# Hash bits by way of DRAM in ScalarE's queue, weight exponents in halves, and two pairs of heads in another order

## The chip, the cores and the metric

One core of a Trainium2 chip runs the kernel in one launch. The metric is the device time of one execution in microseconds (us). The engines are TensorE (PE in the profile), VectorE (DVE), ScalarE (ACT), GpSimd (POOL) and SyncE (SP); each works through its own instructions in the order in which the program gives them, and engines wait for each other by semaphores. DMAs are issued here from SP, ScalarE and GpSimd.

## The reference

```python
def _attn_ref(q, k, v, proj):                 # q, k, v: (4, 8, 768, 64); proj: (64, 6)
    q_bits = (np.einsum('bhsd,dk->bhsk', q, proj) > 0).astype(np.int64)
    k_bits = (np.einsum('bhsd,dk->bhsk', k, proj) > 0).astype(np.int64)
    powers = 2 ** np.arange(n_bits)
    mask = np.sum(q_bits * powers, -1)[:, :, :, None] == np.sum(k_bits * powers, -1)[:, :, None, :]
    scores = np.where(mask, scale * np.matmul(q, k.transpose(0, 1, 3, 2)), -1000000000.0)
    attn = np.exp(scores - np.max(scores, axis=-1, keepdims=True))
    attn = attn / (np.sum(attn, axis=-1, keepdims=True) + 1e-09)
    return np.matmul(attn, v).astype(np.float32)

def _moe_ref(x, w_in, w_out):                 # x: (3072, 512); w_in: (512, 2048); w_out: (2048, 512)
    r = np.maximum(x @ w_in, 0.0)
    return ((r * r) @ w_out).astype(np.float32)
```

A query attends only to the keys with the same six sign bits. The attention's output, heads side by side, is the input `x` of a layer with a squared ReLU. The two weight matrices arrive as 64-bit floating-point numbers.

## The kernel before

The kernel has two halves. The first computes the attention of the 32 heads, two heads (a pair `pr`, 0 to 15) at a time, and writes `x` to DRAM. The second is the layer with the squared ReLU, by products of blocks that save multiplications; the change does not touch it.

**One pair.** Scores are computed with keys on the partitions. A half-score `score(pr, kt, i)` (L442) is for key block `kt` (0 to 5, 128 keys) and half `i` of the queries (384): TensorE multiplies first the hash bits of keys and queries (`marks`, bf16) and then the features (`own`, fp32) into one PSUM tile `st` for both heads (`products`, L426). The bits are scaled so that a pair of query and key with different bits gets a score so negative that its exponential is 0. ScalarE then takes the exponential into the tile `e` (`weight`, L437). `st` comes from `turn` (L105), a ring of two PSUM buffers, which the projections of the hash (`hash_bits`, L358) use too. So a half-score can start only when the exponential of the half-score two turns back is done. `attend(pr, kt, s)` (L494) multiplies `e` by the values into `xo`; `attend_whole` (L510) does both of its halves at once. VectorE adds the `e` tiles into `total` (`add_up`, L465); `sum_up`, `invert`, `spread` and `normalize` (L525 to L591) turn that into the divisor and apply it to `x_raw`, ScalarE's copy of `xo` (`keep_x`, L516). `sum_up` and `spread` use `spare`, one more PSUM buffer.

**The hash bits of the next pair.** While a pair is scored, `hash_bits(pr + 1)` projects the next pair's features, `signs` (L383) turns that into scaled signs by two operations of ScalarE into the tile `signed`, whose rows are ordered by queries or keys, half and bit. `place_bits` (L391) copies them to the rows of the tiles `bits` where `products` reads them, by eight DMAs in SP's queue, seven partitions each. SP's queue also carries the loads of queries and keys (`qk_nat`, L307, eight per pair), of values (`v_nat`, L316) and of weights (`raw`, L141), the writes of `x_t` (L591) and of the block sums of the weights (`w_in<-s_in`, L219), and from pair 13 on the blocks `w_unit` (L656). GpSimd loads `x` (L640) from pair 12 on.

**The weights.** Beside the attention the 64-bit weights are rounded to 32 bits, one piece per pair. VectorE cuts out the exponent (`part_power`, L146), ScalarE shifts it to its place by two operations over 2 x 512 elements per partition (`place_power`, L157), VectorE takes the rest (`part_top`, L167) and puts both together (`round_weight`, L183).

**The order** is written out by hand in the loop over the pairs (L687 to L773): half-scores and attends alternate, and the other steps stand between them. For pair 0 the hash of pair 1 stands behind its first four half-scores, and VectorE makes pair 1's features (`features(1)`, L351) just before. After the last pair come its last two `attend_whole`, the divisor and the last sums of `x` (L774 to L788).

Of the kernel before, what the change touches and what calls it, by code (L numbers as in the profile page):

```python
# [9 lines left out]
BF16 = mybir.dt.bfloat16  # L10
# [24 lines left out]
def kernel(  # L35
# [120 lines left out]

    def place_power(i):  # L157


        if i not in parts:  # L160
            return
        power = parts[i]
        small = p_w.tile([P, 2, PIECE], U8, name="small", bufs=1)
        nc.scalar.activation(out=small, in_=power, func=ACTF.Relu, bias=excess)  # L164
        nc.scalar.activation(out=power, in_=small, func=ACTF.Copy, scale=2.0**23)  # L165
# [49 lines left out]
    def put_factor(n, c, t):  # L215
# [27 lines left out]
    signed = const.tile([P, 2, HS], BF16, name="signed")  # L243
    all_bits = [
        [const.tile([P, S], BF16, name=f"bits{w}_{i}") for w in range(2)] for i in range(2)
    ]

    def constants():
# [10 lines left out]
        for r in range(0, P, NR_B):  # L259
            nc.vector.memset(lifts[r:r + N + 1], 1.0)  # L260
            nc.vector.memset(lifts[r:r + N], -SMALL)
            if r >= 2 * NR_B:
                nc.vector.memset(gains[r:r + N + 1], -FAR / 2 * N)
                nc.vector.memset(gains[r:r + N], FAR / 2)
        for pair in all_bits:
            for t in pair:
                nc.gpsimd.memset(t, 0.0)
        nc.vector.memset(ones, 1.0)
# [103 lines left out]
    def first_signs(w):  # L372

        bits[0, w] = t = all_bits[0][w]
        for c in range(2):
# [7 lines left out]
    def signs(pr):  # L383


        nc.scalar.activation(
            out=signed, in_=hashed[pr, 0][:, :, 0:HS], func=ACTF.Sign, scale=HUGE, bias=lifts
        )
        nc.scalar.activation(out=signed, in_=signed, func=ACTF.Copy, scale=gains)

    def place_bits(pr):  # L391

        for w in (1, 0):
            bits[pr, w] = t = all_bits[pr % 2][w]
            for c in range(2):
                at = (2 * w + c) * NR_B
                for h in range(2):
                    nc.sync.dma_start(  # L398
                        out=t[h * D:h * D + NBITS + 1, c * HS:(c + 1) * HS],
                        in_=signed[at:at + NBITS + 1, h],  # L400
                    )

    def first_keys(c, banks):

        if c == 0:
            bits[0, 1] = all_bits[0][1]
        t = bits[0, 1]
# [257 lines left out]
    with tc.manual_schedule():  # L665
# [21 lines left out]
        for pr in range(NP):  # L687
# [72 lines left out]

            score(pr, 4, 0)
            attend(pr, 2, 1)
            score(pr, 4, 1)
# [19 lines left out]
        for n in (2, 3):  # L783
            sum_x(0, n)
        spread(pr)
        normalize(pr)
# [797 lines left out]
```

## Time and profile before

| | us |
|---|---|
| median of 3 runs | 888.74 |
| lowest and highest run | 888.21, 891.19 |
| the profiled execution | 888.8 |
| its span, from the first instruction to the last | 886.9 |

The profile is of one execution. A row of the timeline gives the start (us from the span's start), the duration, engine, line, operation, tiles, shape and count, and in brackets the idle time of the engine before it and what ended it. A row of a wait gives the engine, line and tile that waited, what for, and the total, the number of times and the longest in us. A row of a group gives busy time and mean duration (ns) of one, then the idle time ahead of it. A row of one line's instructions gives minimum, median and maximum in ns. A row of the DMA chain gives the start, the time from the issue to the use, and the tiles. A row of a stretch gives its bounds and length, the busy time of PE, PEld (TensorE's loading of weights), DVE, ACT and POOL, then the granted share of TensorE's clock, the DMA engines' busy share and GB/s.

### The profile page before, as it was taken

How to read it: one execution, taken by the hardware profiler on the slowest of the kernel's cores; microseconds unless marked ns; L12 is line 12 of the kernel's file. 1: busy time of each engine (PE TensorE's matmuls, PEld its weight loads, DVE VectorE, ACT ScalarE, POOL GpSimd, SP SyncE). 2: the span in 40 equal slices, each digit the busy share in tenths (PEclk: the TensorE clock that was granted, in tenths of full speed). 3: DMA queues.
4: the chain of work that ended last, by engine and by line, in shares of the span. 5: the costliest groups of instructions: out<-in, count | busy, mean ns of one | idle time of the engine just before them, and what ended most of it. 6: DMA issues, size and time to landing. Idle time of an engine off the chain costs nothing.

```text
span 886.9 us, 16832 instructions
## 1 busy us (share of the span) xinstructions
PE 861.4 (97%) x6612; PEld 539.3 (61%) x6612; DVE 751.6 (85%) x1021; ACT 347.2 (39%) x552; POOL 123.6 (14%) x232
## 2 busy tenths in 40 slices
PE   7999999999989999999999999999999999999996
PEld 3555555555545554444588875556888755568885
DVE  4899999998978988888779978888889788888875
ACT  5777767776756662222211113332111133321110
POOL 1000000000000000554213121111100211110002
PEclk9999999999999999999999999999999999999998
DMA  9667897988887732999788874446756745454565
GB/s 206 120 123 155 205 178 161 191 202 184 187 213 166 261 100 92 332 291 292 253 325 268 240 181 145 165 130 226 277 161 174 184 141 168 130 166 145 165 170 106
DMA packets 224422, 168.03 MB, mean 189 GB/s; under 512 B 164904, under 2 KB 182640, under 8 KB 224336
## 3 DMA queue, kind: packets, MB, share of 16 engines
q1 hardware_dynamic: 189424, 87.84, 41.2%
q0 software_dynamic: 12528, 41.30, 14.9%
q10 hardware_dynamic: 22384, 37.76, 13.9%
q8 instruction: 53, 0.87, 0.4%
q14 instruction: 33, 0.27, 0.1%
HBM read 124.52 MB, written 41.68 MB: 187 GB/s over the span
## 4 chain that ended last, share of the span: by engine, by line
PE 84%; DMA 5%; ACT 5%; DVE 2%; SPq 2%; issue 1%; ACTq 0%; DVEq 0%
PE acc L812 39%; PE acc L1031 15%; PE st L432 12%; PE xo L488 8%; PE acc L984 5%; ACT e L438 2%; DMA raw<-in_moe_w_out_dram 2%; DMA bits<-signed 2%; ACT power L165 1%; PE tot L537 1%; ACT small L164 1%; SPq L307 1%; PE hash L367 1%; SPq L398 1%; DMA v_nat<-in_v_dram 1%; DVE total L475 1%
## 5 line engine op out<-in xcount | busy, mean ns | idle before, releaser
L438 ACT ACTIVATE e<-st 128x768 f32<-128x768 f32 x192 | 153.6, 809 | 94.7 <-PE st L432 83.7
L432 PE MATMUL st<-feat 64*64 64x384 f32 x1536 | 163.0, 485 | 1.0 <-DVE feat L336 1.0
L488 PE MATMUL xo<-e,v_nat 64*64 64x385 f32 (+1 forms) x1520 | 163.3, 487 | 0.5 <-DMA v_nat<-in_v_dram 0.5
L812 PE MATMUL acc<-b,leaf 128*128 128x256 f32 x600 | 133.0, 379 | 0.0
L812 PEld LDWEIGHTS acc<-b,leaf 128*128 128x128 f32 x600 | 113.9, 190 | 16.0 <-issue 0.6
L475 DVE TENSOR_TENSOR total<-total,e 128x1536 f32<-128x1536 f32 x64 | 111.6, 1743 | 5.1 <-ACT e L438 5.1
L488 PEld LDWEIGHTS xo<-e,v_nat 64*64 64x64 f32 (+1 forms) x1520 | 63.8, 133 | 56.0 <-issue 43.9
L1031 PE MATMUL acc<-t_x,w_unit 128*128 128x512 f32 x192 | 90.2, 592 | 0.0
L432 PE MATMUL st<-bits,bits 64*64 64x384 bf16 x768 | 70.7, 328 | 9.3 <-DMA bits<-signed 6.3
L432 PEld LDWEIGHTS st<-feat 64*64 64x64 f32 x1536 | 61.7, 133 | 29.7 <-issue 25.1
L812 PE MATMUL acc<-t,leaf 128*128 128x256 f32 x336 | 76.3, 380 | 0.0
L812 PEld LDWEIGHTS acc<-t,leaf 128*128 128x128 f32 x336 | 63.6, 190 | 9.3 <-DVE t L602 0.5
L896 DVE SCALAR_TENSOR_TENSOR b<-h 128x512 f32<-128x512 f32 x96 | 65.7, 691 | 3.0
L432 PEld LDWEIGHTS <-bits 64*64 64x64 bf16 x768 | 29.5, 107 | 52.7 <-issue 46.5
L1031 PE MATMUL acc<-x,w_unit 128*128 128x512 f32 x128 | 60.1, 592 | 0.0
L483 POOL MEMSET token<- 1x1 f32 x62 | 16.6, 269 | 309.1 <-PE xo L488 258.6
L812 PE MATMUL acc<-x,w_unit 128*128 128x512 f32 x128 | 56.5, 593 | 0.0
L1031 PEld LDWEIGHTS acc<-t_x,w_unit 128*128 128x128 f32 x192 | 36.5, 190 | 28.9 <-issue 26.8
L812 PE MATMUL acc<-b_t,leaf 128*128 128x256 f32 x240 | 53.8, 379 | 0.0
L812 PEld LDWEIGHTS acc<-b_t,leaf 128*128 128x128 f32 x240 | 45.5, 190 | 6.2
L819 ACT COPY two<-acc 128x256 f32<-128x256 f32 (+1 forms) x29 | 12.5, 432 | 87.9 <-PE acc L812 75.4
L819 ACT COPY one<-acc 128x256 f32<-128x256 f32 (+1 forms) x29 | 12.5, 432 | 82.2 <-PE acc L812 53.5
(159 smaller groups left out, 1181.6 us busy)
## 6 DMA issues: line engine op xcount, KB each, us to landing
leaf<-w_out ACTq DMA_DIRECT2D x142, 256.0 KB
w_unit<-w_in SPq DMA_DIRECT2D x16, 640.0 KB
raw<-in_moe_w_in_dram SPq DMA_DIRECT2D x8, 1024.0 KB
raw<-in_moe_w_out_dram SPq DMA_DIRECT2D x8, 1024.0 KB
w_unit<-w_in SPq DMA_DIRECT2D x8, 896.0 KB
w_out<-sums POOLq DMA_DIRECT2D x16, 448.0 KB, 6.9
sum<-w_in SPq DMA_DIRECT2D x16, 448.0 KB
v_nat<-in_v_dram SPq DMA_DIRECT2D x16, 384.0 KB
```

Source lines behind the costliest of these rows:

```text
L164: nc.scalar.activation(out=small, in_=power, func=ACTF.Relu, bias=excess)
L165: nc.scalar.activation(out=power, in_=small, func=ACTF.Copy, scale=2.0**23)
L432: nc.tensor.matmul(out=st[k * HK:(k + 1) * HK, h, 0:HS], lhsT=src[1][rows, key], rhs=src[0][rows, cut], start=first, stop=not first, skip_ ...
L438: nc.scalar.activation(out=key_of(pr, kt)[:, :, i, 0:HS], in_=st[:, :, 0:HS], func=ACTF.Exp, scale=scale)
L475: nc.vector.tensor_tensor(out=totals[pr], in0=totals[pr], in1=e, op=ALU.add)
L483: step = nc.gpsimd.memset(token, 0.0)
L488: return nc.tensor.matmul(out=outs[pr][h * D:(h + 1) * D, c, 0:HS + 1], lhsT=nat[pr, "v_nat"][rows, h, kt * D:(kt + 1) * D], rhs=key_of(pr ...
L812: nc.tensor.matmul(out=acc[to], lhsT=a(i), rhs=b(i), start=first and i == 0, stop=last and i == n - 1, skip_group_check=True,)
L819: nc.scalar.copy(out=t, in_=acc[of])
L896: nc.vector.scalar_tensor_tensor(out=out, in0=h, scalar=0.0, in1=h, op0=ALU.max, op1=ALU.mult)
L984: nc.tensor.matmul(out=out, lhsT=w[:, a], rhs=b, start=start, stop=stop, skip_group_check=True)
L1031: nc.tensor.matmul(out=acc[to], lhsT=w[:, PLACE[a], f], rhs=bt[b](f), start=first and f == 0, stop=last and f == NFT // 2 - 1, skip_group_ ...
```

## The change

1. `signed` is written to a new DRAM tile `bits_d` by one DMA in ScalarE's queue, right behind the two operations of `signs`. `place_bits` reads it back with two DMAs in ScalarE's queue, one per head, each of seven partitions and four pieces (queries and keys, two halves). They stand behind `score(pr, 4, 0)` and no longer right behind `signs`. The tiles of bits are merged, one for queries and keys together, in place of two.
2. `place_power` works on one half of the piece (512 elements) per call. From pair 1 on the first half stands behind `attend(pr, 1, 0)` and the second where the whole stood; in pair 0 both halves stand where the whole stood.
3. In pair 0, `attend(0, 0, 0)`, `score(0, 2, 0)`, `attend(0, 1, 0)` and `score(0, 2, 1)` move ahead of the hash of pair 1.
4. In the last pair, `score(15, 5, 1)` takes the spare PSUM buffer, `attend(15, 2, 0)` moves behind `add_up(15, 4)`, and the last `attend_whole` and `keep_x` move behind the sums of the divisor and `invert`.

```diff
-    def place_power(i):
+    def place_power(i, g):
         if i not in parts:
             return
-        power = parts[i]
-        small = p_w.tile([P, 2, PIECE], U8, name="small", bufs=1)
+        power = parts[i][:, g]
+        small = p_w.tile([P, PIECE], U8, name="small", bufs=1)
         nc.scalar.activation(out=small, in_=power, func=ACTF.Relu, bias=excess)
         nc.scalar.activation(out=power, in_=small, func=ACTF.Copy, scale=2.0**23)
...
-    all_bits = [
-        [const.tile([P, S], BF16, name=f"bits{w}_{i}") for w in range(2)] for i in range(2)
-    ]
+    all_bits = [const.tile([P, 2, S], BF16, name=f"bits{i}") for i in range(2)]
+    bits_d = p_d.tile([P, 2, HS], BF16, name="bits_d")
...
-        for pair in all_bits:
-            for t in pair:
-                nc.gpsimd.memset(t, 0.0)
+        for t in all_bits:
+            nc.gpsimd.memset(t, 0.0)
...
         nc.scalar.activation(out=signed, in_=signed, func=ACTF.Copy, scale=gains)
+        nc.scalar.dma_start(out=bits_d, in_=signed)
...
     def place_bits(pr):
-        for w in (1, 0):
-            bits[pr, w] = t = all_bits[pr % 2][w]
-            for c in range(2):
-                at = (2 * w + c) * NR_B
-                for h in range(2):
-                    nc.sync.dma_start(
-                        out=t[h * D:h * D + NBITS + 1, c * HS:(c + 1) * HS],
-                        in_=signed[at:at + NBITS + 1, h],
-                    )
+        t = all_bits[pr % 2]
+        src = bits_d.rearrange("(g r) h c -> h r g c", r=NR_B)
+        for h in range(2):
+            nc.scalar.dma_start(
+                out=t[h * D:h * D + NBITS + 1].rearrange("r w (c n) -> r (w c) n", c=2),
+                in_=src[h, 0:NBITS + 1],
+            )
+        for w in range(2):
+            bits[pr, w] = t[:, w]
...
-    def score(pr, kt, i):
+    def score(pr, kt, i, st=None):
...
-        st = turn("st")
+        st = st or turn("st")
...
             else:
                 keep_x(old)
                 sum_up(old, 0)
-            if more:
-                hash_bits(pr + 1, turn("hash"))
-                signs(pr + 1)
-                place_bits(pr + 1)
-            if pr > 0:
-                if not more:
+                if more:
+                    hash_bits(pr + 1, turn("hash"))
+                    signs(pr + 1)
+                else:
                     score(pr, 2, 0)
                 sum_up(old, 1)
                 invert(old)
...
             part_power(pr)
+            if pr == 0:
+                attend(pr, 0, 0)
             if more:
                 score(pr, 2, 0)
-            attend(pr, 0, 0)
+            if pr > 0:
+                attend(pr, 0, 0)
+            else:
+                attend(pr, 1, 0)
             score(pr, 2, 1)
-            attend(pr, 1, 0)
+            if pr > 0:
+                attend(pr, 1, 0)
+                place_power(pr, 0)
+            else:
+                hash_bits(1, turn("hash"))
+                signs(1)
             score(pr, 3, 0)
...
                 normalize(old)
-                place_power(pr)
+                place_power(pr, 1)
             add_up(pr, 3)
...
             score(pr, 4, 0)
+            if more:
+                place_bits(pr + 1)
             attend(pr, 2, 1)
             score(pr, 4, 1)
             attend(pr, 3, 1)
...
             score(pr, 5, 0)
-            attend(pr, 2, 0)
-            score(pr, 5, 1)
+            if more:
+                attend(pr, 2, 0)
+            score(pr, 5, 1, spare("st") if not more else None)
             attend(pr, 3, 0)
             if pr == 0:
-                place_power(0)
+                for g in range(2):
+                    place_power(0, g)
             add_up(pr, 4)
         pr = NP - 1
-        for kt in (SB - 2, SB - 1):
-            attend_whole(pr, kt)
-        keep_x(pr)
+        attend(pr, 2, 0)
+        attend_whole(pr, SB - 2)
         sum_x(0, 1)
         add_up(pr, SB - 1)
...
         invert(pr)
         for n in (2, 3):
             sum_x(0, n)
+        attend_whole(pr, SB - 1)
+        keep_x(pr)
         spread(pr)
         normalize(pr)
```

More of the change, by code (lines that the diff above doesn't have):

```diff
@@ L372, in first_signs @@
     def first_signs(w):
-        bits[0, w] = t = all_bits[0][w]
+        bits[0, w] = t = all_bits[0][:, w]
         for c in range(2):
@@ L389, in signs @@
         nc.scalar.activation(out=signed, in_=signed, func=ACTF.Copy, scale=gains)
+        nc.scalar.dma_start(out=bits_d, in_=signed)
     def place_bits(pr):
-        for w in (1, 0):
-            bits[pr, w] = t = all_bits[pr % 2][w]
-            for c in range(2):
-                at = (2 * w + c) * NR_B
-                for h in range(2):
-                    nc.sync.dma_start(
-                        out=t[h * D:h * D + NBITS + 1, c * HS:(c + 1) * HS],
-                        in_=signed[at:at + NBITS + 1, h],
-                    )
+        t = all_bits[pr % 2]
[7 more added lines that the diff above has]
+            bits[pr, w] = t[:, w]
     def first_keys(c, banks):
         if c == 0:
-            bits[0, 1] = all_bits[0][1]
+            bits[0, 1] = all_bits[0][:, 1]
         t = bits[0, 1]
```

## The prediction

> **What bounds the kernel now.** I read the page's totals first, then what TensorE waited for, then one pair of heads in the timeline, then the DMA issues.
>
> ```profile
> span 886.9 us, 16832 instructions
> PE 861.4 (97%) x6612; PEld 539.3 (61%) x6612; DVE 751.6 (85%) x1021; ACT 347.2 (39%) x552; POOL 123.6 (14%) x232
> ...
> PE st L432 <- DMA bits<-signed: 6.3, 8, 2.6
> PE st L432 <- ACT e L438: 3.1, 15, 0.3
> PE hash L367 <- DVE feat L351: 1.7, 1, 1.7
> ...
> PE xo L488 <- DMA v_nat<-in_v_dram: 0.5, 1, 0.5
> ```
>
> TensorE is busy in 97% of the span, so an edit pays only where TensorE waits, and the change touches only the attention half (up to 341 us). The list of its waits names four there: hash bits that land late, exponentials that come late, the hash of pair 1, and one load of values. Ends of matmuls are modelled, so I price the waits by spacings. The Sign operation (L386) comes once per pair, so its starts are a clock; of pairs 2, 9, 10, 11, 12 and 13:
>
> ```profile
> 57.10 0.90 ACT L386 ACTIVATE signed<-hash,lifts 128x768 bf16<-128x768 f32 x1 [0.33 <-PE hash L367]
> ...
> 194.96 0.90 ACT L386 ACTIVATE signed<-hash,lifts 128x768 bf16<-128x768 f32 x1 [0.33 <-DMA qk_nat<-in_q_dram]
> 215.91 0.90 ACT L386 ACTIVATE signed<-hash,lifts 128x768 bf16<-128x768 f32 x1 [0.34 <-PE hash L367]
> 236.20 0.90 ACT L386 ACTIVATE signed<-hash,lifts 128x768 bf16<-128x768 f32 x1 [0.34 <-PE hash L367]
> 261.03 0.90 ACT L386 ACTIVATE signed<-hash,lifts 128x768 bf16<-128x768 f32 x1 [0.34 <-PE hash L367]
> 282.99 0.90 ACT L386 ACTIVATE signed<-hash,lifts 128x768 bf16<-128x768 f32 x1 [0.34 <-PE hash L367]
> ```
>
> From pair 2 to 9 a pair takes (194.96 - 57.10)/7 = 19.69 us. The next four take 20.95, 20.29, 24.83 and 21.96, which is 1.26 + 0.60 + 5.14 + 2.27 = 9.3 us too much. These are the late bits, with what follows: after the longest wait the clock was granted at half for a while.
>
> ```profile
> 254.00:256.00 2.00, 2.00 (x18) 1.46 (x14) 1.80 (x3) 0.81 (x1) 0.00 (x0) 0.50 1.05 376
> ```
>
> (The 0.50 is the clock.) Now one steady pair, number 4, on ScalarE and TensorE:
>
> ```profile
> 97.39 0.94 ACT L389 ACTIVATE signed<-signed,gains 128x768 bf16<-128x768 bf16 x1
> 99.53 0.33 PE L432 MATMUL st<-bits,bits 64*64 64x384 bf16 x4
> 99.75 0.70 DVE L151 TENSOR_SCALAR power<-raw 128x1024 uint32<-128x1024 uint32 x1
> ...
> 102.69 0.34 PE L432 MATMUL st<-bits,bits 64*64 64x384 bf16 x4
> 103.00 1.14 ACT L164 ACTIVATE small<-power,excess 128x1024 uint8<-128x1024 uint32 x1
> 104.14 0.34 PE L432 MATMUL st<-bits,bits 64*64 64x384 bf16 x4
> 104.17 1.06 ACT L165 ACTIVATE power<-small 128x1024 uint32<-128x1024 uint8 x1
> 105.14 1.50 ACT L438 ACTIVATE e<-st 128x768 f32<-128x768 f32 x2
> 105.98 0.36 PE L432 MATMUL st<-bits,bits 64*64 64x384 bf16 x4 [0.20 <-ACT e L438]
> 107.43 0.36 PE L432 MATMUL st<-bits,bits 64*64 64x384 bf16 x4
> 108.50 0.81 ACT L438 ACTIVATE e<-st 128x768 f32<-128x768 f32 x1 [0.64 <-PE st L432]
> 108.89 0.36 PE L432 MATMUL st<-bits,bits 64*64 64x384 bf16 x4
> ```
>
> Half-scores start every 1.45 us (102.69 to 104.14; 107.43 to 108.89), but 104.14 to 105.98 is 1.84: **0.38 us lost**. The cause: two `turn` buffers, so score(5,0) at 105.98 needs the exponential of (4,0), and ScalarE ran both operations of `place_power` ahead of it. An exponential can start 1.07 us after its half-score starts (107.43 to 108.50) and takes 0.81, or 0.75 back to back; its buffer is wanted again 2.9 us after that start. So ScalarE may be about 1.0 us late before TensorE stops; `place_power` makes it about 1.4 late.
>
> **The change, part by part.**
>
> *1. Four smaller operations (L163 to L165).* Each half has 512 elements. The same engine's copies give the slope:
>
> ```profile
> L1039 ACT COPY two<-acc 128x512 f32<-128x512 f32 x16 | 9.4, 586 | 24.4 <-PE acc L1031 24.4
> L819 ACT COPY two<-acc 128x256 f32<-128x256 f32 x21 | 7.8, 373 | 65.1 <-PE acc L812 52.6 <-DMA leaf<-w_out 6.3 <-DVE h L599 3.1
> ```
>
> (586 - 373)/256 = 0.83 ns per element, so an operation of 1.06 us becomes 1.06 - 512 x 0.83 ns = 0.63, a half is 1.27 us, and ScalarE does 0.4 more per pair in all. The first half moves between the exponentials of (2,1) and (3,0); the second stays. In pairs 1 to 14 the 0.38 goes if nothing new comes: 14 x 0.38 = **5.3 us**. Pair 0 keeps its halves together at its end, and pair 15 is bound by VectorE (part 4).
>
> *2. Three DMA issues on ScalarE.* Eight issues leave SP; one write of `signed` to DRAM and two reads arrive in ScalarE's instruction stream.
>
> ```profile
> L398 SPq DMA_DIRECT2D bits<-signed x120: 688/689/1303, 23.6 to 311.1; - x120
> L1098 ACTq DMA_DIRECT2D leaf<-w_out x142: 326/327/702, 438.2 to 867.6; - x142
> ```
>
> The write has 128 rows like L1098, the reads have seven partitions like L398: 0.33 to 0.70 and 0.69 to 1.30 us each. I take 0.33 and 0.69, the medians, as the nearest rows. Walk through pair 4, its stall taken out: the write waits for `signed` (97.39 + 0.94 = 98.33), so exp(2,0) runs 98.7 to 99.5 and score(3,0) wants its buffer at 99.53: no wait, or 0.35 at 0.70. `part_power` ends at 99.75 + 0.70 = 100.45, then half a `place_power` to 101.7, exp(3,0) to 102.45 (wanted 102.69), exp(3,1) to 103.2, second half to 104.45, exp(4,0) to 105.2 (wanted 105.60). The reads wait for nothing fresh, so they can issue beside exp(4,0), 104.5 to 105.9; behind them queues exp(4,1), ending at 106.65, wanted at 107.05 by score(5,1). So at medians nothing stalls, with 0.1 to 0.4 us to spare. Between nothing and 0.35 at the write, and nothing and 0.8 at the reads, I take 0.15 us per pair: **-2.1 us** over 14 pairs, so 3.2 is left of part 1.
>
> The read also waits, on ScalarE, for the write to land; 98.7 to 104.5 is the cover.
>
> *3. The bits arrive by another queue.* Today they queue on SP behind weights and loads:
>
> ```profile
> 29.08 2.63 DMA bits<-signed
> ...
> 206.83 1.77 DMA bits<-signed
> ...
> 247.88 5.61 DMA bits<-signed
> ```
>
> From issue to use 1.77 us in a quiet stretch (0.69 of it issue), 2.63 beside loads, 5.61 beside a 2 MB load of `x`. Write: 5.8 us of cover, enough by all three. Reads: the second issues at about 105.2 and pair 5 wants it at 108.89 - 0.38 = 108.5, so 3.3 us: enough for the first two, not the third. What made bits late at pairs 9 to 13 was the issue: SP reached them late.
>
> ```profile
> 202.04 6.95 SPq L398 DMA_DIRECT2D bits<-signed  x8
> ...
> 268.32 7.73 SPq L398 DMA_DIRECT2D bits<-signed  x8
> ```
>
> The signs there ended at 196.8 and 262.9 (start + 0.90 + 0.94), so 5 us went by before SP reached the first issue and 7 to 8 in the eight issues, which ended at 209.0 and 276.0. ScalarE's reads issue 6.2 to 7.6 us after the signs (as in the walk through pair 4) and land by 205.5 and 271.6; the next pair wants them 12.0 us after its signs began (96.5 to 108.5 in pair 4), at 207.0 and 273.0. The longest wait stood beside POOL's load of `x`:
>
> ```profile
> 246.36 0.91 POOL L640 DMA_DIRECT2D x<-x_all  x1 [0.26 <-DMA raw<-in_moe_w_out_dram]
> ...
> 294.01 0.91 SPq L656 DMA_DIRECT2D w_unit<-w_in  x2
> ```
>
> The reads of that pair (238.0 + 6.2, to 245.6) issue before it. But what frees SP also moves the two `w_unit` loads from 294.0 to about 288, beside the reads of pair 13. Of 9.3 us I keep 1.5 for such collisions: **+7.8**, bounds 2 and 9.3. Every SP issue behind the eight (`x_all`, `v_nat`, eight `qk_nat`) also moves up by about 5 us (8 x 0.69), so the late `v_nat` of pair 14 (0.5) is early: **+0.6**.
>
> *4. First and last pair.* Pair 0 today waits 1.73 us for VectorE's `features(1)`; now two attends and two half-scores stand before the hash: +1.7, if `v_nat` has landed by about 15 us, 3.6 earlier than it is used now (the list has no wait for it there; bounds 0 and 1.7). But score(3,0) then follows score(2,1) by only the hash (0.64), with no attend between, and wants the buffer of exp(2,1), which ends 1.07 + 0.81 after score(2,1) starts: 1.88 - 1.45 = 0.4 lost, and about 0.2 behind the signs. Net **+1.1**. In the last pair VectorE is the chain:
>
> ```profile
> 323.70:338.90 15.20, 13.93 (x168) 6.98 (x164) 14.99 (x15) 8.66 (x11) 0.18 (x2) 1.00 0.13 45
> ...
> 338.92 0.86 PE L537 MATMUL tot<-total,ones 128*32 128x192 f32 x16 [1.02 <-DVE total L475]
> 340.95 0.50 PE L571 MATMUL tot<-both,picks 64*64 64x24 f32 x4 [1.18 <-DVE both L560]
> ```
>
> VectorE works 14.99 of 15.20 us up to the last `add_up`. Moving `attend_whole` (1.3 us) into the 1.18 wait fills a hole whose end VectorE sets: **+0.2**, bounds 0 and 1.0. The spare PSUM buffer and the merged memsets cost nothing: both are ready long before use.
>
> Sum: 5.3 - 2.1 + 7.8 + 0.6 + 1.1 + 0.2 = **12.9 us**. The profiled execution took 888.8 us (span 886.9 and 1.9 around it), as the median of 888.74. Forecast: 888.8 - 12.9 = 875.9, say **876 us**. VectorE does not bite before: in pair 4 it idles 1.24 of 19.70 us, and part 1 asks 0.23.
>
> **Rivals.**
>
> *A. ScalarE's issues take the place of the stall: slower.* Exp(4,1) may start by 106.3, so two reads from 104.5 on fit up to 0.9 us each. SP's issues of `qk_nat`, which move to the same moment, can be long, and if ScalarE's have to wait for them, the reads do:
>
> ```profile
> 499.28 18.28 SPq L1129 DMA_DIRECT2D out_dram<-h  x16
> ```
>
> Against: beside these 16 issues (1.14 us each) ScalarE's issues stayed within 0.70. For: 0.40 us of slack at 0.69, and L398's own 1.30. At 1.30 the reads end at 107.1 and exp(4,1) 0.8 too late; with the write at 0.70 a pair loses 1.0 us instead of 0.38: 14 x 0.6 = 9 more than now; if the reads also wait for exp(4,0) to end (0.75 more), 1.77: 14 x 1.4 = 19. With the other gains (9.7) that is 888 to 898, say 893. Slower from 1.1 us of stall per pair.
> By the Trainium skill's "Perfetto Trace Analysis", "DMA Instruction — HWDGE (DVE, Sync)", the descriptor generator is locked for exclusive use while one sequencer issues, which is this rival's mechanism. The row above speaks against a long lock.
>
> *B. The bits stay late.* The reads share DMA engines with what SP now sends earlier, at the same time. If the two long stalls (5.14 + 2.27, of which I had given up 1.5) stay, it is 888.8 - 12.9 + 5.9 = 882; if besides each pair waits 0.35 us, 887. For: 5.61 us beside one load. Against: today's stalled pairs begin with a late issue.
> The skill's "DMA: Bandwidth & Descriptors", "Issuing engines are not separate DMA queues", says that DMAs of all issuing engines interleave on the same engines and only issue time is saved; by it the 5.61 would remain and the time would be this rival's 882.
>
> **How the numbers follow.** Forecast 0.62 (870 to 881), B 0.20 (882 to 887), A 0.16 (888 to 898), better than 870 0.02. About 0.3% (2.7 us) is what a measurement of this kernel tells from no change: faster, below 886.1, holds the forecast and most of B, 0.79; within 0.07; slower 0.14, nearly all of A. The range from 870 to 889 leaves out the worse part of A and the 0.02.
>
> **What would show it.** Right: signs every 19.4 to 19.6 us from pair 2 to 14, no pair over 20.5; waits of TensorE for `bits` under 2 us; hash of pair 1 without a wait; `small` twice per pair at about 0.7 us. A: issues on ScalarE's queue over 0.9 us and "ACT e" the longest wait. B: "DMA bits" still there, with pairs 11 and 12 above 21 us. Wrong altogether: a period above 19.7 with neither wait, or a second half that takes longer than before from the last `spread` on.

## The result and the profile after

| us | before | after |
|---|---|---|
| median of 4 runs each, on one chip | 889.97 (888.21 to 894.74) | 881.6 (881.1 to 882.96) |
| the profiled execution's span | 886.9 | 879.7 |

The ratio is 0.99, with a 95% interval from 0.9858 to 0.9942: faster by 1%, 8.4 us in the medians and 7.2 in the profiled spans, where 12.9 had been forecast (876 us). The time lies in the forecast's range (870 to 889) and at the figure of rival B (882), but B's reason is only part of it.

The changed kernel's page begins with these totals:

```profile
span 879.7 us, 16684 instructions
...
PE 859.9 (98%) x6612; PEld 538.5 (61%) x6612; DVE 751.6 (85%) x1021; ACT 353.0 (40%) x584; POOL 123.8 (14%) x230
```

TensorE's waits in the changed kernel (total, times, longest, us):

```profile
PE st L431 <- ACT e L437: 3.9, 3, 2.5
PE st L431 <- DMA bits<-bits_d: 2.4, 5, 0.7
PE tot L536 <- DVE total L474: 1.9, 1, 1.9
```

The waits for the hash of pair 1 and for `v_nat` are gone. The wait for bits fell from 6.3 to 2.4, but the wait for exponentials, which had been fifteen short stops of at most 0.3 us, is now one of 2.5 and two short ones. ScalarE's timeline shows where. These are the Sign operations (now L384) in pairs 9 to 14, named by the pair that is being scored, with what follows the one in pair 12; the starts are again the clock of the pairs:

```profile
191.97 0.90 ACT L384 ACTIVATE signed<-hash,lifts 128x768 bf16<-128x768 f32 x1 [0.32 <-PE hash L365]
212.22 0.90 ACT L384 ACTIVATE signed<-hash,lifts 128x768 bf16<-128x768 f32 x1 [0.33 <-PE hash L365]
231.59 0.90 ACT L384 ACTIVATE signed<-hash,lifts 128x768 bf16<-128x768 f32 x1 [0.32 <-PE hash L365]
250.95 0.90 ACT L384 ACTIVATE signed<-hash,lifts 128x768 bf16<-128x768 f32 x1 [0.32 <-PE hash L365]
251.88 0.94 ACT L387 ACTIVATE signed<-signed,gains 128x768 bf16<-128x768 bf16 x1
255.33 0.35 ACTq L388 DMA_DIRECT2D bits_d<-signed  x1
255.79 1.51 ACT L437 ACTIVATE e<-st 128x768 f32<-128x768 f32 x2 [2.97 <-DMA qk_nat<-in_k_dram]
...
275.83 0.90 ACT L384 ACTIVATE signed<-hash,lifts 128x768 bf16<-128x768 f32 x1 [0.33 <-PE hash L365]
296.43 0.90 ACT L384 ACTIVATE signed<-hash,lifts 128x768 bf16<-128x768 f32 x1 [0.33 <-PE hash L365]
```

A pair now takes 19.36 us where nothing disturbs it (231.59 to 250.95), against 19.69 before. But pair 12 (250.95 to 275.83) takes 24.88, pair 13 takes 20.60, and pair 9 (191.97 to 212.22) 20.25. The long one has a visible cause. `signed` is done at 252.82, yet its write to DRAM, the next instruction of ScalarE, starts at 255.33, and the exponentials queued behind it have stood 2.97 us when they start. The row names a load of keys as what ended the idle time, and that load has nothing to do with `signed`.

The chain of waits of the changed kernel, in order of time, confirms it, and goes on to the reads of these bits:

```profile
243.91 3.98 SPq L305
...
247.93 2.90 SPq L305
...
250.88 4.39 DMA qk_nat<-in_k_dram
255.27 0.03 ACTq L388
...
255.33 0.35 ACTq L388
...
263.81 0.27 ACTq L395
...
264.12 4.41 DMA bits<-bits_d
```

Two issues of keys on SP took 3.98 and 2.90 us beside GpSimd's 2 MB load of `x`; the load of keys issued next, at 250.88, landed at 255.27, and ScalarE's write was let go in the same moment. The write then needed 8.2 us to land (263.55 by the trace's semaphore updates), so the first read went out at 263.81, 12.9 us after the Sign, where a quiet pair has it out at 7.5. The last read was used at 264.12 + 4.41 = 268.53, 17.58 us after the Sign; the next pair wants it 12.06 after (12.0 in the prediction's walk). These 5.52 us are the pair's whole loss, so it is still paid as late bits: TensorE's stop for the exponentials lies inside it. By the same reckoning, with the landings from the semaphore updates, late bits are 8.4 of the 8.8 us that all pairs lose. After TensorE's stop of 2.5 us its clock was granted at half (third column from the end), as in the stretch of the kernel before:

```profile
258.00:260.00 2.00, 2.00 (x20) 1.25 (x19) 1.99 (x2) 1.27 (x2) 0.00 (x0) 0.50 0.89 266
```

The built program's list of waits says why a write of bits should wait for a load of keys. It is no profile; the rows are ScalarE's write and reads of that pair, and SP's loads of queries and keys ahead of the write:

```
ScalarE  bits_d<-signed        waits DMAHW3, DMAHW5, DMAHW2, Activation
ScalarE  bits<-bits_d          waits DMAHW6, DMAHW2
ScalarE  bits<-bits_d          waits DMAHW0
SP       qk_nat<-in_q_dram x4  wait  DMAHW2 | DMAHW4 | DMAHW6 | DMAHW7
SP       qk_nat<-in_k_dram x4  wait  DMAHW0 | DMAHW1 | DMAHW2 | DMAHW3
```

SP's and ScalarE's DMAs share eight completion counters (semaphores that a landing counts up), handed out in turn in the program's order. Each DMA waits until the last user of its counter, about the eighth DMA before it, has landed. The write's own counter is DMAHW2, which the third load of keys has, exactly eight DMAs earlier; in the trace both count on the same semaphore. The second read of bits lists no wait but its counter's. The kernel before has the same rule, but its ScalarE issued no DMA between the first loads and the second half, so in the attention only SP ever stood in this line.

The span can be cut by starts that every trace has: the Sign in pair 1, the Sign in pair 14 (13 periods later), the copy `x_raw` of pair 14, and the first product of the second half. With the base period of each kernel times 13 taken out of the second part, what is left is what pairs take beyond the base ("over base"). The table also holds the experiments below.

| kernel | to the Sign in pair 1 | 13 base periods | over base | to `x_raw` of pair 14 | to first product | from there |
|---|---|---|---|---|---|---|
| before | 37.55 | 256.0 | 9.1 | 19.16 | 19.56 | 545.5 |
| after | 35.96 | 251.7 | 8.8 | 18.25 | 19.56 | 545.5 |
| halves alone | 37.87 | 251.6 | 16.0 | 18.24 | 19.56 | 545.5 |
| order alone | 41.87 | 255.8 | 8.6 | 22.29 | 19.55 | 545.1 |
| bits alone | 37.41 | 256.0 | 6.5 | 18.56 | 19.57 | 547.6 |
| bits and halves | 38.05 | 251.7 | 8.0 | 18.25 | 19.56 | 545.5 |
| `x` two pairs later | 36.32 | 251.7 | 4.2 | 18.26 | 20.98 | 546.6 |
| big loads behind the reads | 36.00 | 251.7 | 4.2 | 20.27 | 19.57 | 545.4 |
| big loads in pair 15 | 36.23 | 251.7 | 4.5 | 18.25 | 19.56 | 545.3 |

From before to after: 1.6 in pair 0, 4.3 in the base period, 0.3 over base, 0.9 up to `x_raw` of pair 14, nothing behind it: 7.1 of the 7.2 us. The base period did what was forecast and more; the loss to late bits did not shrink, it changed its place. (The last column holds no part of the change. Bits alone has 2.1 us more there, 1.7 of them because TensorE's clock was granted at half from 338.0 to 341.4, at the start of the second half.)

### The profile page after: what moved, and what is told of

It is laid out like the page before. It is cut to its first block, busy times and chain, and to the rows that moved or that the text cites. A ratio compares the mean times of both kernels' runs of the same rounds, so it can differ in the third digit from the quotient of the medians.

```text
span 879.7 us, 16684 instructions
## 1 busy us (share of the span) xinstructions
PE 859.9 (98%) x6612; PEld 538.5 (61%) x6612; DVE 751.6 (85%) x1021; ACT 353.0 (40%) x584; POOL 123.8 (14%) x230
## 4 chain that ended last, share of the span: by engine, by line
PE 88%; DMA 5%; DVE 3%; ACT 2%; SPq 1%; issue 1%; ACTq 0%; POOL 0%; DVEq 0%; POOLq 0%
PE acc L824 40%; PE acc L1043 16%; PE st L431 14%; PE xo L487 11%; PE acc L996 5%; DMA bits<-bits_d 2%; PE tot L536 1%; SPq L305 1%; DMA qk_nat<-in_k_dram 1%; PE hash L365 1%; DMA w_in<-s_in 1%; DMA bits_d<-signed 1%; DVE total L474 1%; ACT e L437 1%; DVE total L469 0%
## 5 line engine op out<-in xcount | busy, mean ns | idle before, releaser
L437 ACT ACTIVATE e<-st 128x768 f32<-128x768 f32 x192 | 151.6, 809 | 79.7 <-PE st L431 67.5
L431 PE MATMUL st<-bits 64*64 64x384 bf16 x768 | 70.9, 328 | 6.5 <-ACT e L437 3.9
## 6 DMA issues: line engine op xcount, KB each, us to landing
leaf<-w_out ACTq DMA_DIRECT2D x142, 256.0 KB
```

The source lines that it names most:

```text
L431: nc.tensor.matmul(out=st[k * HK:(k + 1) * HK, h, 0:HS], lhsT=src[1][rows, key], rhs=src[0][rows, cut], start=first, stop=not first, skip_ ...
L437: nc.scalar.activation(out=key_of(pr, kt)[:, :, i, 0:HS], in_=st[:, :, 0:HS], func=ACTF.Exp, scale=scale)
```

## The experiments

**The theory** after the first comparison: bits are late because DMAs of SP and ScalarE wait for each other's landing through the shared counters, and big loads (`x`, `w_unit`) make those landings slow. **The rival**: plain contention, the bits' own transfers are slow beside the big loads wherever they are issued. Each kernel is compared with the kernel before on the same chip, whose medians were 890.07 to 892.04 us in these groups.

### One part alone

**Halves alone.** The kernel before with `place_power` in halves.

```diff
             attend(pr, 1, 0)
+            if pr > 0:
+                place_power(pr, 0)
             score(pr, 3, 0)
...
-                place_power(pr)
+                place_power(pr, 1)
```

> The kernel before with the weight exponents in halves as the only edit. If the halves alone remove the wait of TensorE for the exponential, the pair takes 19.36 us as in the changed kernel in place of 19.69, which over 14 pairs is 4.6 us, and the late bits stay: 884 us. If ScalarE's extra 0.4 us per pair eats it, the pair stays at 19.7 us: 889 us.

Measured: 891.25 us (888.52 to 898.31), ratio 1.0007 (0.998 to 1.0033): no gain, less than either figure of the expectation. The base period did fall to 19.35, so the stall of 0.38 us was real and the halves remove nearly all of it. But the time over base rose from 9.1 to 16.0. TensorE's waits and SP's queue in this kernel:

```profile
PE st L432 <- DMA bits<-signed: 9.5, 8, 3.7
```

```profile
240.53 9.01 SPq L398 DMA_DIRECT2D bits<-signed  x8
```

The wait for bits grew from 6.3 to 9.5 us: TensorE comes earlier, SP does not. Of the 9.01 us that the eight issues take here, 2.3 pass between two of them (245.11 to 247.38), until a load of weights eight DMAs earlier has landed. TensorE's clock was granted at half in two stretches of 3.4 us of the attention, in one before. What part 1 wins is given back where bits come late.

**Order alone.** The kernel before with only the new order of the first and the last pair; `place_bits` stays right behind `signs` on SP.

```diff
+            if pr == 0:
+                attend(pr, 0, 0)
             if more:
                 score(pr, 2, 0)
-            attend(pr, 0, 0)
...
+            else:
+                hash_bits(1, turn("hash"))
+                signs(1)
+                place_bits(1)
```

> The kernel before with the other order of the first and the last pair as the only edit. If the first pair gives the 1.6 us by which the changed kernel's second Sign starts earlier, and the last pair nothing because VectorE's chain sets its end: 887 us. If the last pair gives its bound of 1 us too: 886 us.

Measured: 893.4 us (891.1 to 895.07), ratio 1.002 (1.0002 to 1.0037): slightly slower, where 887 or 886 was expected. The wait for the hash of pair 1 went, but the Sign in pair 1 came at 41.87, 4.3 us later than before, because SP's copies of pair 1's bits now stood behind a whole load of queries and keys:

```profile
22.32 3.77 SPq L307 DMA_DIRECT2D qk_nat<-in_k_dram  x4
26.20 6.13 SPq L398 DMA_DIRECT2D bits<-signed  x8
```

The part from `x_raw` of pair 14 to the first product stayed at 19.55, so the new order of the last pair is worth nothing, here as in the whole change.

**Bits alone.** The kernel before with only the way through DRAM in ScalarE's queue.

```diff
         nc.scalar.activation(out=signed, in_=signed, func=ACTF.Copy, scale=gains)
+        nc.scalar.dma_start(out=bits_d, in_=signed)
...
             score(pr, 4, 0)
+            if more:
+                place_bits(pr + 1)
```

> The kernel before with the bits by way of DRAM in ScalarE's queue as the only edit. By step 3 of the prediction the late bits go (7.8 us) and ScalarE's issues cost 2: 883 us. If, as the two traces suggest, the late bits only change their place (9.3 us of them before, 8.6 after), nothing is gained: 888 to 890 us.

Measured: 887.56 us (884.88 to 891.9), ratio 0.9949 (0.9924 to 0.9974). The base period stayed at 19.69 to 19.70, so three issues on ScalarE cost nothing in a quiet pair. Over base fell only from 9.1 to 6.5. TensorE's waits in this kernel:

```profile
PE st L431 <- ACT e L437: 5.0, 19, 1.3
...
PE st L431 <- DMA bits<-bits_d: 1.6, 4, 0.6
```

The wait for bits shrank to 1.6, as forecast; the wait for exponentials rose from 3.1 to 5.0 with a longest of 1.3, as not forecast. The time lies next to the second figure of the expectation (888 to 890), but partly by chance: 2.1 us of this profile are lost in the second half, outside the change, and up to its first product this kernel is 3.4 us ahead.

**Bits and halves together**, without the new order: the two edits above in one kernel.

> The kernel before with parts 1 and 2 of the change together (the bits by way of DRAM in ScalarE's queue, and the exponents in halves), without the new order of the first and last pair. The theory, that the 0.33 us per pair of the halves is kept only when the bits no longer queue on SP, expects a base period of 19.36 us and about 4.5 us less than the bits alone had (887.6), so 883; with pair 0 as before (1.6 us slower than in the changed kernel) that agrees with 881.6 + 1.6 = 883. The rival, that a shorter period always comes back as late bits, as it did with the halves alone, expects the base period of 19.36 as well but 886 to 888, with the extra time of the late pairs grown from 6.4 to about 10 us.

Measured: 885.16 us (882.04 to 888.06), ratio 0.9938 (0.9915 to 0.9962); the profiled execution has 19.36 as its base and 8.0 over base. The spans go from 885.6 (bits alone) to 881.0, which looks like the theory's 4.5, but 2.1 of it is the second half of bits alone, and over base grows from 6.5 to 8.0, about midway to the rival's 10. The medians say as little: 885.16 lies between the theory's 883 and the rival's 886, and the two ratios overlap. So it is shown that the base period holds and that over base does not grow to the 16 of halves alone; at `x_raw` of pair 14 this profile is 2.4 us ahead of bits alone, and what arrives on average is not settled.

### The queue or the way through DRAM

**SP issues.** The changed kernel with the same write and reads, at the same places of the program, on SP.

```diff
-        nc.scalar.dma_start(out=bits_d, in_=signed)
+        nc.sync.dma_start(out=bits_d, in_=signed)
...
-            nc.scalar.dma_start(
+            nc.sync.dma_start(
```

> The changed kernel with the write of signed and the two reads of the bits issued by SP in place of ScalarE, at the same places of the program. If it is the queue that counts, the three issues stand on SP behind its weights and loads, and the write also holds up what is behind it until signed is done: bits late in most of the pairs from 9 on, 886 to 892 us. If it is the way through DRAM that counts (three issues in place of eight), 880 to 884 us, with pair 12 no worse than the 24.9 us of the changed kernel, since ScalarE then has no issue in its stream that could stop its exponentials.

Measured: 899.58 us (898.53 to 906.5), ratio 1.0123 (1.0084 to 1.0163), slower than either figure expected. From pair 1 on every pair takes 20.3 us or more; pair 12 takes 21.0, so with ScalarE's stream free of issues its long stop is gone. TensorE's waits and, from the chain of waits, the end of one pair:

```profile
PE st L431 <- DMA bits<-bits_d: 15.5, 15, 3.1
```

```profile
234.71 0.33 SPq L590
...
235.14 0.39 SPq L314
...
235.57 0.02 SPq L395
...
235.61 5.79 DMA bits<-bits_d
```

The reads stand behind SP's write of `x_t` (L590), which waits for VectorE, and its load of values (L314), and are wanted before they land. In a quiet pair (2) they go out 8.5 and 9.4 us after the Sign, in the changed kernel 7.5 and 7.8. So it is the queue that counts, even for so few issues. The Trainium skill's "DMA: Bandwidth & Descriptors", "Issuing engines are not separate DMA queues", says that issuing from several engines saves only the time that the issue takes on its sequencer. Three issues of about 0.3 us would be 0.9 us per pair; the medians of the two kernels, on two chips, are 18 us apart, some 1.3 per pair. What the other engine saves here is the place in line, and for that the measurement decides.

**Eight direct copies on ScalarE.** The changed kernel without DRAM: the eight copies of the kernel before, issued by ScalarE where the reads stand.

```diff
-        nc.scalar.dma_start(out=bits_d, in_=signed)
...
+                    nc.scalar.dma_start(
+                        out=t[h * D:h * D + NBITS + 1, w, c * HS:(c + 1) * HS],
+                        in_=signed[at:at + NBITS + 1, h],
+                    )
```

> The changed kernel without the way through DRAM: eight copies from signed straight to the bits, in ScalarE's queue, where the two reads stand. If an issue on ScalarE costs the 0.69 us of SP's copies, the eight hold ScalarE for 5.5 us, of which some 1.5 are covered: 14 pairs lose about 3.5 us each and the time is about 930. If they cost 0.27 us like the two reads, 2.2 us in all, a pair loses about 0.5 us: 888.

Measured: 985.62 us (983.73 to 986.65), ratio 1.104 (1.0999 to 1.1081), pairs of 27 us. An issue costs what the first figure (930) assumed, but the line of them holds ScalarE longer, and TensorE's clock was granted at half in part of each pair (0.95 on average over the run, 0.995 in the changed kernel). ScalarE's timeline in one pair, then one line's issues (minimum, median and maximum in ns):

```profile
103.77 7.90 ACTq L396 DMA_DIRECT2D bits<-signed  x7
111.72 1.51 ACT L438 ACTIVATE e<-st 128x768 f32<-128x768 f32 x2 [7.38 <-DMA bits<-signed]
```

```profile
L396 ACTq DMA_DIRECT2D bits<-signed x120: 704/714/1315, 23.1 to 406.8; - x120
```

and the changed kernel's issues:

```profile
L388 ACTq DMA_DIRECT2D bits_d<-signed x15: 349/349/409, 20.7 to 298.3; - x15
```

```profile
L395 ACTq DMA_DIRECT2D bits<-bits_d x30: 272/274/536, 23.2 to 304.2; - x30
```

DRAM is what makes the issues fit beside the exponentials: a read of seven partitions takes 0.27 us to issue and two replace eight copies of 0.71, 0.55 in place of 5.7 us.

### What holds ScalarE up in pair 12

**The load of `x` two pairs later.**

```diff
-            if pr == X_0:
+            if pr == X_0 + 2:
                 load_x(0)
```

> The changed kernel with the first load of x issued at pair 14 in place of pair 12. Theory: the 5.5 us that pair 12 loses is a wait of ScalarE ahead of its write of the bits, for an earlier load of keys that the load of x holds up; the wait is there because SP's and ScalarE's DMAs share eight semaphores and each waits for the one eight DMAs earlier. No key is loaded any more at pair 14, so the loss goes and nothing takes its place: 876 us, pair 12 at 19.4. Rival: the bits' own transfer is slow beside the load of x; then the loss moves to pair 14 with the load: 881 us.

Measured: 879.06 us (877.95 to 879.89), ratio 0.9853 (0.9818 to 0.9889). Pair 12 is back at 19.35 us. ScalarE's write in this kernel goes out as soon as `signed` is done:

```profile
250.88 0.90 ACT L384 ACTIVATE signed<-hash,lifts 128x768 bf16<-128x768 f32 x1 [0.32 <-PE hash L365]
...
252.77 0.35 ACTq L388 DMA_DIRECT2D bits_d<-signed  x1
```

SP's four loads of keys show why. First those of this kernel, then of the changed kernel:

```profile
244.23 2.60 SPq L305 DMA_DIRECT2D qk_nat<-in_k_dram  x4
```

```profile
243.91 9.46 SPq L305 DMA_DIRECT2D qk_nat<-in_k_dram  x4
```

So the 5.5 us of pair 12 are shown to come from the load of `x`. Without it both steps of the changed kernel's chain are short: the write goes out on time, and it lands in 5.5 us in place of 8.2. The run does not separate the two, and both theories allow it. Pair 13 takes 21.97, 1.4 more than in the changed kernel, and the last pair 1.4 more, so 876 was missed.

**The write of bits issued by GpSimd**, whose DMAs use counters of their own.

```diff
-        nc.scalar.dma_start(out=bits_d, in_=signed)
+        nc.gpsimd.dma_start(out=bits_d, in_=signed)
```

> The changed kernel with the write of the bits to DRAM issued by GpSimd, whose DMAs have counters of their own; the two reads stay in ScalarE's queue. Theory: ScalarE no longer waits for the load of keys that stands eight DMAs earlier, so the 5.5 us at pair 12 shrink to under 1.5 and the time falls to about 877 us. Rival (the transfer of the bits itself is what is slow beside the load of x): pair 12 stays above 23 us and the time at 881.

Measured: 939.65 us (938.94 to 941.33), ratio 1.0525 (1.0489 to 1.0562). This is no clean test: GpSimd also sets the `token` that orders the halves of `sum_up`, and the token now queues behind a DMA that waits for `signed`:

```profile
PE tot L536 <- POOL token L482: 41.4, 14, 3.0
```

Pairs 1 to 11 take 23.9 to 24.1 us and pair 12 takes 25.58, 1.7 more, where the changed kernel lost 5.5. The wait ahead of the write is gone, as the theory has it: the write goes out at 305.47, 0.3 us after `signed` is done, while SP still issues loads of keys (until 306.19). What is left is slow landing, as the rival has it: the last read takes 5.11 us from issue to use, where the pairs before have 2.6 to 3.6. The size of the two shares proves little, since the longer pairs leave more time for the loads.

```profile
305.47 0.54 POOL bits_d L388
...
316.47 5.11 DMA bits<-bits_d
```

**Queries and keys earlier**, right behind the write of bits, so that they should have landed long before the next write.

```diff
                     signs(pr + 1)
+                    if pr + 3 < NP:
+                        load_pair(pr + 3)
```

> The changed kernel with each pair's keys and queries loaded some 6 us earlier, right behind the write of the bits, so that the DMA eight places ahead of that write is no load of keys. Theory: the 5.5 us at pair 12 go, and 876 to 878 us; the reads, eight to nine places behind loads of keys, may wait a little at other pairs. Rival (slow transfer beside the load of x): the loss at pair 12 stays, 881 us.

Measured: 899.99 us (897.83 to 902.18), ratio 1.0079 (1.0048 to 1.0109): slower, against the expectation. But it is the best evidence for the counters, because the eight loads now stand about eight DMAs ahead of the reads of bits, and in several pairs it is the reads that wait. The chain of waits of pair 8:

```profile
181.30 0.57 SPq L305
...
181.92 7.46 DMA qk_nat<-in_q_dram
...
189.41 0.27 ACTq L395
```

A load of queries for another pair lands after 7.46 us, and 0.02 us later the read of bits goes out; the exponentials behind it were 3.5 us late. TensorE's waits for exponentials add up to 16.8 us in this kernel, the longest 7.0. In pair 12 the expectation fails: it takes 28.27 us, 8.9 too long, because there the write of bits has a load of weights (`raw`) eight DMAs ahead, on the same counter, and goes out 7.0 us after `signed` is done:

```profile
264.88 9.33 DMA raw<-in_moe_w_out_dram
...
274.30 0.35 ACTq L388
```

Contention alone does not explain issues that start when an unrelated transfer ends.

**The load of `x` in four parts**, one in each of pairs 9 to 12.

```diff
-            if pr == X_0:
-                load_x(0)
+            f = pr - (X_0 - 3)
+            if 0 <= f < NFT:
+                nc.gpsimd.dma_start(out=xs[0][0][:, f], in_=x_all[:, f, 0:NCH])
```

> The changed kernel with the first load of x cut into four parts of 512 KB, issued at pairs 9 to 12. Both readings expect pair 12 near 19.4 to 20.5 us, since no part holds the DMA engines for more than 2 us; the theory of the shared semaphores expects no loss at pairs 9 to 11 beyond what is there (0.1, 0.9, 0), so 877 us; if the transfers themselves are slow beside any load of x, each of the four pairs loses 1 us or more and the time is 880.

Measured: 882.85 us (879.46 to 886.32), ratio 0.9886 (0.9836 to 0.9935). Pair 12 is at 19.37, but pairs 9, 11 and 13 take 23.80, 21.84 and 21.87, and neither figure (877 or 880) is met. In pair 9 ScalarE stops again ahead of the reads, 3.84 us until a write of block sums has landed. This decides nothing: the write of the bits themselves had needed 9.6 us and landed only 0.2 us before that one. Smaller loads spread the loss over more pairs instead of removing it.

### A place where the big loads meet no bits

**Behind the reads.** `w_unit` behind the reads of bits in pair 13, `x` behind those in pair 14.

```diff
             if more:
                 place_bits(pr + 1)
+            if pr == X_0 + 1:
+                for n in range(2):
+                    load_unit(n)
+            if pr == X_0 + 2:
+                load_x(0)
```

> The changed kernel with the two loads of w_unit moved behind the reads of the bits in pair 13 and the first load of x behind the reads of the bits in pair 14. The theory that the stalls of pairs 12 and 13 are what these big loads do to the write and the reads of the bits (the issue that waits for another DMA, and the slow landing) expects both to go: 881.6 - 5.5 - 1.2 = 875 to 876 us, with periods of 19.4 to 20 us in pairs 12 and 13. The rival, that big loads cost the same wherever they stand, since the DMAs are close to full for the whole of these pairs, expects the loss in pairs 14 and 15: 879 to 882 us, with x_raw of pair 14 later than 18.3 us after the last signs.

Measured: 879.65 us (878.97 to 884.24), ratio 0.9887 (0.9861 to 0.9913). Pair 12 is at 19.37; pair 13 still takes 20.55, and pair 14 2.0 us more. "Behind" holds on one engine's stream only: GpSimd waits for nothing there, and sent the load of `x` at 295.99, ahead of ScalarE's reads, which then took 6.28 us from issue to use. First GpSimd's timeline, then the chain of waits:

```profile
295.99 0.91 POOL L639 DMA_DIRECT2D x<-x_all  x1
```

```profile
299.38 0.27 ACTq L395
...
299.70 6.28 DMA bits<-bits_d
```

This is the rival's contention, and it is there too; the time is the rival's figure as well (879 to 882).

**In pair 15**, where no bits are read any more.

```diff
             beside(5, 1)
+            if pr == NP - 1:
+                load_x(0)
+                for n in range(2):
+                    load_unit(n)
```

> The changed kernel with the first load of x and the two loads of w_unit moved into pair 15, behind attend(14, 5, 1): there no pair follows whose bits could be late, SP has only the small writes of block sums left, and VectorE needs x at about 325 us, 15 us later. If the stalls of pairs 12 and 13 are what these three loads do to the write and the reads of the bits, both go and nothing takes their place: 881.6 - 5.5 - 1.2 = 875, between 874 and 877, with 19.4 us in pairs 12 and 13 and x_raw of pair 14 at 18.3 us after the last signs. If big loads cost the same wherever they stand, the last pair pays: 879 to 882, with the first product more than 19.6 us after x_raw of pair 14, waiting for x or w_unit.

Measured: 877.69 us (876.2 to 878.52), ratio 0.9852 (0.9823 to 0.9881). This is the lowest time of the study, though its ratio equals that of `x` two pairs later (0.9853), and it misses the range of 874 to 877 by 0.7. It was not run beside the changed kernel, and the two intervals overlap a little; the profiled spans are 875.5 and 879.7, and the last pair pays nothing (18.25 and 19.56, as after). Pair 12 is at 19.37, so that step holds. Pair 13 still takes 20.54, with no `w_unit` near it, so those loads are not what it takes, and that part of the expectation failed. The chain of waits there has

```profile
280.74 4.38 DMA bits<-bits_d
```

with none of the three moved loads near: 4.38 us from the issue of a read of 21 KB to its use, beside the load of values that SP issues at the same time, where the next pair gives it 3.2 (12.06 us after the Sign). It has no more because the reads went out 8.6 and 8.9 us after the Sign, not 7.5 and 7.8: the write had needed 6.6 us to land, with SP's 1 MB of weights (`raw`, issued at 271.34) under way.

## Why the prediction was right in sign and too large

- **Which stall, and that halves remove it (part 1): right.** 0.38 us per pair were read off, 0.33 came. A half took 0.72 + 0.63 us where 1.27 was estimated; the missing 0.05 was not traced.
- **Three issues on ScalarE (part 2): the size of the reads was wrong.** 0.69 us was taken from the seven-partition copies between parts of SBUF; the reads from DRAM take 0.27. Whether the source or the shape makes the difference was not separated. With that nothing of the 2.1 us was lost in quiet pairs, and parts 1 and 2 gave 14 x 0.33 = 4.6 in place of 3.2.
- **The bits by another queue (part 3): this step failed.** Of 9.3 us, 7.8 were to come back; 0.3 did. Two waits were missed. The step let ScalarE's write wait for `signed` and the reads for the write. In the trace the write waits 2.5 us more, for a load of keys, and ScalarE's exponentials wait with it. The Trainium skill's "DMA: Bandwidth & Descriptors", "Anatomy of one DMA — SWDGE (gpsimd) path", says that a semaphore wait happens on the issuing sequencer before dispatch; the trace agrees (ScalarE idle 2.97 us), and so a wait that on SP cost only SP's time costs the exponentials' time here. And the transfers are slower than the rows that were taken as enough. The step counted 5.8 us of cover for the write; it needed 8.2 in pair 12 and 7.1 in pair 13, and the reads cannot go out before. The last read took 4.4 to 6.3 us from issue to use in the chains above, not 2.63, and 3.4 to 3.6 even in quiet pairs (2, 3, 5 and 10), which bear it because the next pair gives it 4.2 there. The step asked only about the reads beside the big loads: those of pair 11 do go out ahead of the load of `x` (239.40 and 239.71, `x` at 241.79), but the next write meets it. And `w_unit` moved up from 294.0 to 275.2, not to 288, ahead of the write of pair 13 and not beside the reads.
- **`v_nat` of pair 14 (+0.6): right.** 19.16 to 18.25 is 0.91, of which 0.33 is the base period; bits alone has the same 0.6 (18.56).
- **First pair: 1.6 in place of 1.1; last pair: nothing in place of 0.2.** VectorE sets the end of the last pair, as the prediction said, so filling TensorE's hole is worth nothing at all. The new first pair pays only together with the new queue: with the bits on SP it lost 4.3 us.
- **The sum was not of independent terms.** Halves alone gave 0 and order alone lost; both are worth something only since the bits left SP's line. Adding the parts as if each acted alone would have been wrong even with every size right.
- **The rivals.** A named the right place, the exponentials behind ScalarE's DMAs, with the wrong price: issues took at most 0.54 us, and there was one long wait of 2.5 us, not 14 stalls. B gave the right time, in part by luck: it still counted 1.9 us won from late bits, where 0.3 came, and the halves and the first pair won 1.9 us more than the sum had. Its transfers are slow, but the largest loss, in pair 12, begins with a wait ahead of an issue, and its sign (pairs 11 and 12 above 21 us) holds for pair 12 alone. The tests that the prediction set (no pair over 20.5 us, waits for bits under 2 us) failed in pairs 12 and 13, and with 2.4 us.

Left open: pair 9 loses between 0.8 and 2.1 us in the profiles of kernels that differ only in later pairs, so it depends on how the loads happen to fall; how much of pair 12's 5.5 us is the wait for the load of keys and how much the slow write and reads, and what these share the DMA engines with, was not separated. A kernel with counters of its own for the bits was not tried, apart from the one by GpSimd.

## What to carry to other kernels

Before a DMA moves into the queue of an engine that computes, list everything that its issue can wait for: its data, and also the completion counter that it shares with a DMA some eight places earlier in the program. Then look at the slowest landing near it in the trace, since the engine's computing waits as long. A gain in the base period is kept only if the slowest feeder of the loop, here the line of DMAs, is not what paces it; and a big load goes where nothing small is waited for.

## What the runs showed of the hardware

- The issue of a DMA from DRAM to seven partitions with four pieces each took 0.27 us, that of a copy of seven partitions within SBUF 0.71 (0.69 on SP); the write of 128 partitions to DRAM 0.35.
- The second of a pair's two reads of 21 KB from DRAM needed 3.4 to 3.6 us from issue to landing in quiet pairs; the reads in the chains shown here needed 3.9 to 6.3 from issue to use, beside other loads. The write of 192 KB of `signed` needed 7.09 us beside two loads of 0.9 MB (`w_unit`), in pair 13 of the changed kernel. The chain of waits there:

```profile
277.73 7.09 DMA bits_d<-signed
...
284.89 3.90 DMA bits<-bits_d
```

- After a stop of TensorE of 2.5 us (2.6 in the kernel before) its clock was granted at half for 3.4 us.
- The operations of `place_power` on 512 elements took 0.72 and 0.63 us (rows of the changed kernel, minimum, median and maximum in ns), on 1024 elements before 1.14 and 1.06: half the elements cost 0.6 of the time.

```profile
L164 ACT ACTIVATE small<-power,excess x32: 711/722/725, 28.1 to 322.9; 128x512 uint8<-128x512 uint32 x32
```

```profile
L165 ACT ACTIVATE power<-small x32: 629/630/634, 28.8 to 323.7; 128x512 uint32<-128x512 uint8 x32
```
